# Modulation rows in column groups, input products inside the last chunks, and block 2's parameters ahead of the first rows, in an S4 block with an MLP

## The chip, the cores and the metric

The kernel runs on one core of one Trainium2 chip. The metric is the device time of one execution in microseconds (us). Engines are named as the profile names them: PE multiplies matrices, PEld loads its weights, DVE works on vectors, ACT evaluates functions and copies, POOL has little to do here, SP issues DMAs. All instructions of one engine run in their order; between engines semaphores tell when an operand is ready.

## The reference

The input `x` is 2048 × 512, `c` a vector of 512. A vector of six modulation rows is computed from `c`; the rows scale, shift and gate two halves of the block.

```python
mod = (silu(c) @ w_mod).reshape(1, 6, 1, 512)          # six rows of 512
sa, ca, ga, sb, cb, gb = rows of mod
h = layernorm(x) * (1 + ca) + sa
x = x + ga * S4(h)                                     # A part
h = layernorm(x) * (1 + cb) + sb
x = x + gb * (mish(h @ w1 + b1) @ w2)                  # B part

def S4(u):                      # L = 2048, D = 512 channels, N = 128 states
    dt = exp(log_dt); A = A_re + 1j*A_im
    K[d, l] = Re sum_n C[d, n] * exp(dt[d]*A[d, n]*l) * dt[d]*B[d, n]
    y = irfft(rfft(pad(u)) * rfft(pad(K)))[:L]         # causal convolution by FFT of length 2L
    return y + u * Dskip
```

## The kernel before

The 512 channels are four **blocks** of 128. For each block the function `params(b, stage)` (lines 233 to 298), in stages 0 to 5, turns the six parameter planes `raw[b]` (B, C, A, real and imaginary) into four planes of logarithms and angles; stages 0, 2, 3 and 5 are chains of small DVE operations, stage 1 is a logarithm and an exponential on ACT, stage 4 an arctangent on ACT. The result is split into three parts and packed in a tile `pk` (one buffer), stored to DRAM by `store_pk(b)` and read back transposed by `load_s(b)` as `S3` and `S12`. `load_params(b)` loads `raw[b]`.

The convolution kernels are then made in 32 **chunks** of 16 channels, eight per block. One chunk is, in order: `s_ang` (PE, eight matmuls into `pang`), `s_sin` (ACT, three operations into `ec`), `s_mag` and `comb` (DVE, `m` and the four products in `ec`), `s_kgen` (PE, 32 matmuls into `pkg`), `s_ks` (ACT copy `ks`), `s_skip` (DVE), `s_ka` (PE, eight matmuls into `pka`), `s_tm` (ACT copy into `gk`). The steps of one chunk lie in several rounds of the loop at lines 604 to 623: round k holds `s_kgen(k-1)`, `s_ang(k+3)`, `s_ka(k-3)` for PE and so on. Before each eight chunks a `visit(b)` changes ACT's table to exponentials, makes the coefficients `co` of eight chunks (sixteen PE matmuls `pco` and ACT operations) and changes the table back; in visit 1 ACT also does the logarithm and exponential of block 3 as its last operations.

Between these run the rest of the inputs' work: `u_load`, `u_stats`, `u_norm` (layer norm and modulation of the input, on DVE), `u_mm` (first transform, PE), `u_out` (to DRAM `ud`); `mod_mm` and `mod_out`, which make rows 0 to 2 from weights `early` loaded at the start, three rows at a time in three groups of 32 output columns of the array; `gains`, which loads these rows back from DRAM `md` on all partitions (`gs`, `ga`) for `u_norm`; and `mod_row(v)` for rows 3 to 5, one row at a time in one column group, with weights `wm` loaded inside.

**What sets the order.** Four tables, `pe`, `se`, `ve` and `vt` (lines 575 to 602), say in which round each extra step stands. Steps of `ve` are spread between the DVE operations of that round, those of `vt` follow behind. `follow` (line 103) chains everything that goes through `mm`, `act`, `V`, `A` or `load` into one written order per engine; PE's is that of the `mm` calls. DMAs issued by `nc.sync.dma_start` are placed on SP by the scheduler, by priority and by when their buffers are free. In the rows of the profile most lines are those of the helpers (L119, L141, L147, L150), so steps are told apart by tiles.

After the chunks come 16 **products** (`product(q)`, lines 654 to 672): the input's columns `ur` are loaded from `ud`, transformed (PE, `pub`; ACT copy `f`), the kernel's are transformed (PE, `pkb`), multiplied on DVE (`y`), and `inverse(q)` transforms back (PE, `pz`; ACT copy `z`; store to DRAM `zd`). The weights of the MLP are loaded and split meanwhile (`w1s`, `w1h`). The last stage reads `zd`, finishes the inverse, does the second layer norm and the MLP (`pm`, `po`).

Of the kernel before, what the change touches and what calls it, by code (L numbers as in the profile page):

```python
# [84 lines left out]
def s4_block(ctx, tc, io, out):  # L85
# [390 lines left out]
    MQ = {}  # L476

    def load_mq(w):
        for n in ("mf", "mi"):
            t = MQ[n, w] = mip.tile([P, 8, P], F32, tag=n, name=f"{n}{w}")  # L480
            nc.sync.dma_start(t.rearrange("p a b -> p (a b)"), view(io[n], w * 8 * P, [[32 * P, P], [1, 8 * P]]))

    def transform(p, q, rhs):
        for c in range(2):
            for r in range(2):
                T.matmul(p[64 * r:64 * r + 64, c, :], MQ["mf", q // 4][:, 2 * (q % 4) + r, 64 * c:64 * c + 64], rhs(r),  # L486
                         start=True, stop=True)
# [100 lines left out]
    at(se, 10, run, params(3, 4))
    at(ve, 10, params, 3, 5)
    at(se, 11, store_pk, 3)  # L590
    for n, k, d in ((0, 4, ve), (1, 7, vt), (2, 9, ve), (3, 12, ve), (4, 15, vt), (5, 17, ve), (6, 20, ve), (7, 23, vt)):
# [278 lines left out]
```

## Time and profile before

| | us |
|---|---|
| median of three runs | 761.16 (759.93 to 761.22) |
| profiled execution | 760.93 |
| its span | 759.2 |
| PE busy | 649.6 (86%) |
| DVE busy | 431.8 (57%) |
| ACT busy | 318.7 (42%) |
| chunks, first angle matmul to first product | 26.3 to 298.4 |
| products, first `pub` to the end of the stretch shown | 298.4 to 389.7 |
| MLP, last stage | 419.5 to 759.2 |

A row of the trace reads: start and duration, engine, line, operation, written tile <- read tiles, partitions × elements, count of instructions that the row joins; in brackets the idle time of the engine before the row, and what ended it. A chain row has start, length, and what the chain followed there. SPq is the queue of SP, which issues DMAs. The mean granted clock of PE over the span was 0.911 of full speed.

### The profile page before, as it was taken

What the parts mean: (1) busy time and instruction counts of PE and PEld (TensorE: products, weight loads), DVE (VectorE), ACT (ScalarE), POOL (GpSimd) and SP (SyncE); (2) the same over time, 40 slices, a digit from 0 to 9 for tenths busy, and PEclk for the clock granted to TensorE, in tenths of its full rate; (3) what the DMA queues carried; (4) which work ended last, traced back from release to release, by engine and by line L of the source; (5) the groups of instructions that cost most, each with busy time, mean ns of one, the idle gap of its engine ahead of it and who ended that gap; (6) DMA issues with size and microseconds to landing.
All of it is one profiled execution on the core that took longest, in us unless ns stands there. A gap on an engine that the chain in (4) does not pass through costs nothing.

```text
span 759.2 us, 11837 instructions
## 1 busy us (share of the span) xinstructions
PE 649.6 (86%) x4848; PEld 440.8 (58%) x4848; DVE 431.8 (57%) x813; ACT 318.7 (42%) x468; POOL 5.0 (1%) x12
## 2 busy tenths in 40 slices
PE   0319887886988999999944999999999999999996
PEld 0205654663764665233311777888778877888884
DVE  7478786999897692877637724242244424332113
ACT  2156586667867684444321621232223222322220
POOL 2000000000000000000000000000000000000000
PEclk9857796997888699999985899999999999999998
DMA  6712121322422336999449625005220400011002
GB/s 184 258 67 79 43 85 42 116 101 78 126 86 84 140 112 183 251 311 297 166 125 229 163 40 110 1 0 111 55 57 1 92 19 1 0 28 30 0 1 55
DMA packets 34218, 74.56 MB, mean 98 GB/s; under 512 B 5322, under 2 KB 9806, under 8 KB 33652
## 3 DMA queue, kind: packets, MB, share of 16 engines
q1 hardware_dynamic: 33284, 72.17, 33.0%
q10 hardware_dynamic: 576, 1.05, 0.7%
q8 instruction: 38, 0.62, 0.4%
q0 software_dynamic: 304, 0.59, 0.3%
q14 instruction: 16, 0.13, 0.1%
HBM read 49.66 MB, written 24.13 MB: 97 GB/s over the span
## 4 chain that ended last, share of the span: by engine, by line
PE 71%; DVE 14%; DMA 6%; ACT 6%; issue 2%; SPq 1%; ACTq 0%; DVEq 0%
PE pm L759 21%; PE po L776 20%; PE pang L147 5%; DVE ec L119 4%; PE pz L679 4%; PE pub L486 4%; PE pkg L147 3%; PE pkb L486 3%; DVE raw L119 3%; PE pco L147 3%; PE pka L147 2%; PE pia L724 2%; ACT co L141 2%; PE pmod L147 2%; DVE m L119 2%
## 5 line engine op out<-in xcount | busy, mean ns | idle before, releaser
L759 PE MATMUL pm<-hh,w1h 128*128 128x512 f32 x448 | 142.6, 398 | 0.7 <-ACT hh L119 0.7
L141 ACT ACTIVATE mh<-pm,b 128x512 f32<-128x512 f32 x56 | 38.6, 689 | 228.4 <-PE pm L759 228.4
L119 DVE TENSOR_TENSOR mal<-mh,mah 128x512 fp32r<-128x512 f32 x56 | 38.7, 691 | 155.7 <-ACT mah L119 155.3
L759 PEld LDWEIGHTS pm<-hh,w1h 128*128 128x128 f32 x448 | 84.8, 189 | 21.6 <-ACT hh L119 1.5
L776 PE MATMUL po<-w2h,mah 128*128 128x512 f32 x224 | 89.4, 399 | 0.0
L759 PE MATMUL pm<-hh,w1l 128*128 128x512 f32 x224 | 88.8, 397 | 0.0
L776 PE MATMUL po<-w2l,mah 128*128 128x512 f32 x224 | 88.6, 395 | 0.0
L776 PE MATMUL po<-w2h,mal 128*128 128x512 f32 x224 | 88.5, 395 | 0.0
L147 PE MATMUL pang<-ac,s 96*128 96x512 f32 x128 | 55.1, 476 | 26.3 <-DMA s<-pkd 26.3
L119 DVE TENSOR_TENSOR ec<-ec,m 128x1024 f32<-128x1024 f32 x64 | 61.1, 955 | 13.4 <-ACT ec L141 12.7
L147 PE MATMUL pco<-mc,s 64*128 64x384 f32 x64 | 32.6, 604 | 35.2 <-ACT co L141 34.4
L147 PEld LDWEIGHTS pkg<-ec 128*32 128x32 f32 x2048 | 37.6, 120 | 38.4 <-issue 31.1
L147 PE MATMUL pkg<-ec 128*32 128x64 f32 x2048 | 42.5, 241 | 18.9 <-DVE ec L119 5.9
L119 DVE TENSOR_TENSOR y<-pkb,f 128x1024 f32<-128x1024 f32 x32 | 37.7, 1220 | 24.8 <-PE pkb L486 24.8
L776 PEld LDWEIGHTS po<-w2h,mah 128*128 128x128 f32 x224 | 42.1, 188 | 14.6 <-ACT mah L119 4.9
L147 PEld LDWEIGHTS pang<-ac,s 96*128 96x128 f32 x128 | 28.9, 226 | 34.1 <-issue 27.3
L759 PEld LDWEIGHTS pm<-hh,w1l 128*128 128x128 f32 x224 | 42.5, 190 | 10.1
L776 PEld LDWEIGHTS po<-w2h,mal 128*128 128x128 f32 x224 | 42.1, 188 | 10.2
L776 PEld LDWEIGHTS po<-w2l,mah 128*128 128x128 f32 x224 | 42.1, 188 | 9.8
L147 PEld LDWEIGHTS pco<-mc,s 64*128 64x128 f32 x64 | 16.9, 269 | 50.1 <-ACT co L141 47.2
L147 PE MATMUL pang<-am,s 96*128 96x512 f32 x128 | 45.4, 441 | 0.0
L119 DVE TENSOR_TENSOR m<-co 128x1024 f32<-128x1024 f32 x32 | 39.1, 1221 | 7.3 <-ACT co L141 7.3
(96 smaller groups left out, 896.8 us busy)
## 6 DMA issues: line engine op xcount, KB each, us to landing
ud<-u SPq DMA_DIRECT2D x16, 512.0 KB, 2.7
ur<-ud SPq DMA_DIRECT2D x32, 256.0 KB, 5.1
zd<-z SPq DMA_DIRECT2D x16, 512.0 KB, 2.7
zl<-zd SPq DMA_DIRECT2D x28, 256.0 KB, 4.9
x<-in_A_u SPq DMA_DIRECT2D x32, 128.0 KB, 2.9
x<-in_A_u SPq DMA_DIRECT2D x8, 512.0 KB, 6.9
out<-ot SPq DMA_DIRECT2D x32, 128.0 KB, 2.3
w1s<-in_B_w SPq DMA_DIRECT2D x8, 448.0 KB, 6.2
```

Source lines behind the costliest of these rows:

```text
L119: ins = getattr(self.engine, name)(*a, **kw)
L141: follow("act", nc.scalar.activation(out, in_, f, **kw))
L147: follow("pe", T.matmul(out, lhsT, rhs, start=start, stop=stop))
L486: T.matmul(p[64 * r:64 * r + 64, c, :], MQ["mf", q // 4][:, 2 * (q % 4) + r, 64 * c:64 * c + 64], rhs(r), start=True, stop=True)
L679: T.matmul(p[:, r, :], mi[64 * r:64 * r + 64, q % 4, c, :], Y[q][64 * r:64 * r + 64, c, :], start=(c == 0), stop=(c == 1))
L724: T.matmul(p[64 * tl:64 * tl + 64, :], di, ZL[tt, hv][:, j % 2, tl, :], start=True, stop=True)
L759: T.matmul(p, w1[wi][:, k, fs], hh[:, hi, k, :], start=(n == 0), stop=(n == 3 * KB - 1))
L776: T.matmul(PO[tt][q], a[ai][:, P * q:P * q + P], w2[wi][:, f, :], start=(f == 0 and n == 0), stop=(f == FB - 1 and n == 2))
```

## The change

It does five things. First, `load_params(2)` stands behind `load_params(1)` on SP. On SP, at the program's start (`raw2` is block 2's parameters, `pkd` the packed store and `s3`, `s12` its read-back), before:

```order
L438 DMA x0_201<-in_A_u 64x1x512 x4
L438 DMA x1_206<-in_A_u 64x1x512 x4
L438 DMA x2_211<-in_A_u 64x1x512 x3
L150 DMA pkd_75<-pk0_183 128x1536
L438 DMA x2_211<-in_A_u 64x1x512
L632 DMA b1_3014<-in_b1 128x14
L150 DMA s3_0_193<-pkd_75 64x8x128
L150 DMA s12_0_94<-pkd_75 64x4x256
L150 DMA s12_1_95<-pkd_75 64x4x256
L150 DMA raw2_197<-in_par 128x768
L150 DMA early_85<-in_w_mod 128x2x1536 x2
```

and now:

```order
L150 DMA bdk_102<-in_bdk 128x256
L150 DMA raw1_152<-in_par 128x768
L150 DMA raw2_154<-in_par 128x768
L150 DMA da_103<-in_da 128x128
L150 DMA dtap_86<-in_dtap 4x128
L150 DMA di_104<-in_di 128x64
```

The load of `raw2` moved from behind the read-back of block 0 to the sixth place of the queue; all other loads keep their order.

Second, the arctangents of blocks 1 and 2 stand behind the first chunk's sines, stage 5 and the store of block 1 behind the second chunk's, and `u_stats(0)` goes from the set-up into round 1; `mod_mm`, `mod_out` go one round ahead. On ACT, at the start of the chunks, before:

```order
L141 ACTIVATE raw1_152<-raw1_152 128x128
L141 ACTIVATE raw2_197<-raw2_197 128x128
L119 ACTIVATE ec0_337<-pang0_319 128x2x16x32
L141 ACTIVATE ec0_337<-pang0_319 128x2x16x32
L141 ACTIVATE ec0_337<-ec0_337,halfpi_100 128x2x16x32
L119 ACTIVATE ec1_341<-pang1_328 128x2x16x32
L141 ACTIVATE ec1_341<-pang1_328 128x2x16x32
L141 ACTIVATE ec1_341<-ec1_341,halfpi_100 128x2x16x32
```

and now:

```order
L119 ACTIVATE ec0_302<-pang0_284 128x2x16x32
L141 ACTIVATE ec0_302<-pang0_284 128x2x16x32
L141 ACTIVATE ec0_302<-ec0_302,halfpi_100 128x2x16x32
L141 ACTIVATE raw1_152<-raw1_152 128x128
L141 ACTIVATE raw2_154<-raw2_154 128x128
L119 ACTIVATE ec1_308<-pang1_293 128x2x16x32
L141 ACTIVATE ec1_308<-pang1_293 128x2x16x32
L141 ACTIVATE ec1_308<-ec1_308,halfpi_100 128x2x16x32
```

The three operations of `ec0` moved ahead of the two arctangents on `raw1` and `raw2`.

Third, stage 3 of block 3's parameters goes from round 8 to round 9, stages 4 and 5 from round 10 to 11, its store to 12, and `u_norm(2)` from 9 to 10. On DVE, from the last operations of round 7's end on (`m2_8` and `ec8` belong to chunk 8), before:

```order
L119 TENSOR_TENSOR m2_8_1005<-co8_946 128x1024
L119 TENSOR_TENSOR ec8_857<-ec8_857,m2_8_1005 128x32x32
L119 TENSOR_SCALAR raw3_317<-raw3_317 128x128 x2
L119 TENSOR_TENSOR raw3_317<-raw3_317 128x256
L119 TENSOR_TENSOR raw3_317<-raw3_317 128x128
L119 SCALAR_TENSOR_TENSOR raw3_317<-raw3_317 128x128
L119 TENSOR_TENSOR m2_9_1078<-co9_953 128x1024
L119 TENSOR_TENSOR raw3_317<-raw3_317 128x128
L119 TENSOR_SCALAR raw3_317<-raw3_317 128x128
L119 TENSOR_TENSOR raw3_317<-raw3_317 128x128
L119 TENSOR_SCALAR raw3_317<-raw3_317,ldt_79 128x128
L119 TENSOR_TENSOR raw3_317<-raw3_317 128x128 x2
```

and now:

```order
L119 TENSOR_TENSOR m2_8_1005<-co8_946 128x1024
L119 TENSOR_TENSOR ec8_857<-ec8_857,m2_8_1005 128x32x32
L119 BN_STATS bst_1069<-x2_211 128x6 x2
L119 BN_STATS bst_1069<-x3_926 128x6
L119 TENSOR_TENSOR m2_9_1076<-co9_953 128x1024
L119 BN_STATS bst_1069<-x3_926 128x6
L119 BN_AGGR mv_134<-bst_1069 128x2 x2
L119 TENSOR_TENSOR ec8_857<-ec8_857,m2_8_1005 128x16x32
L119 BN_AGGR mv_134<-bst_1069 128x2 x2
L119 TENSOR_SCALAR rsq_1070<-mv_134 128x4
L119 TENSOR_SCALAR rstd_135<-rsq_1070 128x4
L119 SCALAR_TENSOR_TENSOR ec8_857<-ec8_857,m2_8_1005 128x16x32
```

The block 3 operations between the two parts of chunk 8's combination gave their place to the statistics of the inputs `x2` and `x3`.

Fourth, rows 3 to 5 are made together: `mod_piece(k)`, in rounds 27 to 30, does the matmuls of a quarter of the sum for all three rows, in three column groups of one tile `pmq`; `mod_last` copies and stores them. Their weights are loaded in pieces before (`wm_load`), the first four into the buffer of `raw`, the others into that of `u_load`.

Fifth, the matrices `mf`, `mi` are loaded from round 26 on (`second_part`), the first two product inputs in rounds 30 and 31; `pub(0)` stands in round 31 and `pub(1)` behind the last chunk, in the old PSUM pool, and the matmuls of all products go through `mm`, so in written order. On PE, at the end of the chunks, before:

```order
L147 MATMUL pka27_2858<-bdk_102,ks27_2731 64x32x4 x8
L147 MATMUL pmod5_2877<-wm50_2878,sc_133 32x512 x2
L147 MATMUL pmod5_2877<-wm52_2882,sc_133 32x512 x2
L147 MATMUL pkg30_2889<-ec30_2733 32x64 x32
L147 MATMUL pka28_2922<-bdk_102,ks28_2799 64x32x4 x8
L147 MATMUL pkg31_2939<-ec31_2801 32x64 x32
L147 MATMUL pka29_2972<-bdk_102,ks29_2867 64x32x4 x8
L147 MATMUL pka30_2985<-bdk_102,ks30_2931 64x32x4 x8
L147 MATMUL pka31_2996<-bdk_102,ks31_2981 64x32x4 x8
L486 MATMUL pub0_3041<-ur0_3038,mf0_3010 64x512 x4
L486 MATMUL pkb0_3048<-gk_635,mf0_3010 64x512 x4
L486 MATMUL pub1_3062<-ur1_3059,mf0_3010 64x512 x4
```

and now:

```order
L147 MATMUL pka27_2869<-bdk_102,ks27_2760 64x32x4 x8
L147 MATMUL pmq_2688<-wm8_2614,sc_133 32x512
L147 MATMUL pmq_2688<-wm10_2821,sc_133 32x512 x2
L147 MATMUL pkg30_2894<-ec30_2762 32x64 x32
L147 MATMUL pka28_2927<-bdk_102,ks28_2819 64x32x4 x8
L147 MATMUL pub0_2936<-ur0_2883,mf0_2621 64x512 x4
L147 MATMUL pkg31_2955<-ec31_2824 32x64 x32
L147 MATMUL pka29_2988<-bdk_102,ks29_2881 64x32x4 x8
L147 MATMUL pka30_3004<-bdk_102,ks30_2941 64x32x4 x8
L147 MATMUL pka31_3014<-bdk_102,ks31_2997 64x32x4 x8
L147 MATMUL pub1_3024<-ur1_2946,mf0_2621 64x512 x4
L147 MATMUL pkb0_3055<-gk_635,mf0_2621 64x512 x4
```

Whole rows of modulation left the place between `pka27` and `pkg30`, and a quarter of the sum for three rows stands there (three matmuls); `pub0` moved ahead of `pkg31`, `pub1` ahead of `pkb0`.

```diff
@@ -389,16 +389,27 @@
         A.copy(m[0:96], mod["p"][0:96])
         nc.sync.dma_start(md[0:3], m[0:96:32, :])
 
-    def mod_row(v):
-        p = bank(f"pmod{v}")
-        for k in range(KB):
-            if k % 2 == 0:
-                w = io4.tile([P, 2, D], F32, tag="i", name=f"wm{v}{k}")
-                nc.sync.dma_start(w, view(io["w_mod"], k * P * 6 * D + D * v, [[6 * D, P], [P * 6 * D, 2], [1, D]]))
-            mm(p[0:32, :], sc[:, k:k + 1].to_broadcast([P, 32]), w[:, k % 2], start=(k == 0), stop=(k == KB - 1))
-        m = io4.tile([P, D], F32, tag="o", name=f"mrow{v}", bufs=2)
-        A.copy(m[0:32], p[0:32])
-        nc.sync.dma_start(md[v:v + 1], m[0:1])
+    WM = {}
+
+    def wm_load(*pieces):
+        n = len(pieces)
+        t = gen.tile([P, n, D], F32, tag="raw", name="wm", bufs=1) if n > 2 else \
+            io4.tile([P, n, D], F32, tag="i", name=f"wm{pieces[0]}")
+        for i, p in enumerate(pieces):
+            WM[p] = t[:, i]
+            nc.sync.dma_start(WM[p], view(io["w_mod"], p // 3 * P * 6 * D + (3 + p % 3) * D, [[6 * D, P], [1, D]]))
+
+    def mod_piece(k):
+        if k == 0:
+            mod["q"] = psum.tile([P, 512], F32, tag="pu", name="pmq")
+        for v in range(3):
+            mm(mod["q"][32 * v:32 * v + 32, :], sc[:, k:k + 1].to_broadcast([P, 32]), WM[3 * k + v],
+               start=(k == 0), stop=(k == KB - 1))
+
+    def mod_last():
+        m = io4.tile([P, D], F32, tag="o", name="mrow2", bufs=2)
+        A.copy(m[0:96], mod["q"][0:96])
+        nc.sync.dma_start(md[3:6], m[0:96:32, :])
 
 
     def rsqrt(dst, var, n, pool, tag, V=V):
@@ -473,18 +484,37 @@
             A.copy(u[:, g], PU[n, s][g])
         nc.sync.dma_start(view(ud, 2 * (4 * n + s) * 2 * ROW, [[D, P], [4 * 2 * ROW, 2], [1, D]]), u)
 
-    MQ = {}
+    MQ, UR, FQ = {}, {}, {}
 
     def load_mq(w):
         for n in ("mf", "mi"):
-            t = MQ[n, w] = mip.tile([P, 8, P], F32, tag=n, name=f"{n}{w}")
+            t = MQ[n, w] = MQ["pool"].tile([P, 8, P], F32, tag=n, name=f"{n}{w}")
             nc.sync.dma_start(t.rearrange("p a b -> p (a b)"), view(io[n], w * 8 * P, [[32 * P, P], [1, 8 * P]]))
+
+    def second_part():
+        p0.close()
+        MQ["pool"] = left.enter_context(tc.tile_pool(name="mip", bufs=2))
+        load_mq(0)
 
     def transform(p, q, rhs):
         for c in range(2):
             for r in range(2):
-                T.matmul(p[64 * r:64 * r + 64, c, :], MQ["mf", q // 4][:, 2 * (q % 4) + r, 64 * c:64 * c + 64], rhs(r),
-                         start=True, stop=True)
+                mm(p[64 * r:64 * r + 64, c, :], MQ["mf", q // 4][:, 2 * (q % 4) + r, 64 * c:64 * c + 64], rhs(r))
+
+    def ur_load(q):
+        u = UR[q] = io4.tile([P, 2, D], F32, tag="i", name=f"ur{q}")
+        for c in range(2):
+            nc.sync.dma_start(u[64 * c:64 * c + 64].rearrange("p r d -> p (r d)"),
+                              view(ud, c * ROW + 2 * q * D, [[2 * ROW, 64], [1, 2 * D]]))
+
+    def pub(q, pool):
+        FQ[q] = pool.tile([P, 2, 512], F32, tag="pa", name=f"pub{q}", **({} if q < 2 else {"bufs": 1}))
+        transform(FQ[q], q, lambda r: UR[q][:, r, :])
+
+    def pub_out(q):
+        f = io4.tile([P, 2, D], F32, tag="o", name=f"f{q}", bufs=2)
+        A.copy(f, FQ[q])
+        FQ[q] = f
 
 
     def run(*lists):
@@ -502,6 +532,7 @@
     V.tensor_mul(sc, sc, cT)
     load(bdk, io["bdk"].rearrange("p (c x) -> p c x", c=2))
     load_params(1)
+    load_params(2)
     load(da, io["da"])
     load(dtap[0:P:32], io["dtap"].rearrange("t (k m) -> t k m", m=4))
     load(di, io["di"])
@@ -524,7 +555,6 @@
 
     store_pk(0)
     load_s(0)
-    load_params(2)
     for k in range(0, KB, 2):
         load(early[:, k:k + 2], view(io["w_mod"], k * P * 6 * D, [[6 * D, P], [P * 6 * D, 2], [1, 3 * D]]))
     for n in range(3):
@@ -534,13 +564,8 @@
     tables("natural_log_exp_and_others")
     run(params(1, 1), params(2, 1))
     tables("trig_and_small")
-    run(u_stats(0), params(1, 2), params(2, 2))
+    run(params(1, 2), params(2, 2))
     run(params(1, 3), params(2, 3))
-    run(params(1, 4), params(2, 4))
-    run(params(1, 5))
-    store_pk(1)
-    load_params(3)
-
     NG = 8 * NB
     done = set()
 
@@ -565,7 +590,11 @@
     s_ang(0)
     s_ang(1)
     s_sin(0)
+    run(params(1, 4), params(2, 4))
     s_sin(1)
+    run(params(1, 5))
+    store_pk(1)
+    load_params(3)
     run(params(2, 5))
     visit(0, {2: [lambda: step(s_mag, 0), lambda: run(comb(0))], 4: [lambda: step(s_mag, 1)]})
     store_pk(2)
@@ -577,20 +606,21 @@
     def at(d, k, f, *a):
         d.setdefault(k, []).append((f, *a))
 
-    at(pe, 1, mod_mm)
-    at(se, 2, mod_out)
+    at(pe, 0, mod_mm)
...
     at(ve, 3, gains)
     for b in range(NB - 1):
         at(se, 8 * b + 1, load_s, b + 1)
     at(ve, 2, params, 3, 0)
     at(ve, 5, params, 3, 2)
-    at(ve, 8, params, 3, 3)
...
+    at(ve, 9, params, 3, 3)
...
         at(d, k, u_norm, n)
         for s in range(2):
             t = k + 1 + s
@@ -598,10 +628,18 @@
             at(se, t + 1, u_out, n, s)
         if n + 3 < 8:
             at(se, t + 1, u_load, n + 3)
-    for v in range(3):
-        at(vt, NG - 4 + v, mod_row, 3 + v)
-
-    for k in range(NG + 3):
+    for k, pieces in (20, range(4)), (22, (4, 5)), (23, (6, 7)), (26, (8, 9)), (29, (10, 11)):
+        at(se, k, wm_load, *pieces)
+    for k in range(KB):
+        at(pe, NG - 5 + k, mod_piece, k)
+    at(se, NG - 1, mod_last)
+    at(se, NG - 6, second_part)
+    at(se, NG - 2, ur_load, 0)
+    at(se, NG - 1, ur_load, 1)
+    at(pe, NG - 1, pub, 0, psum)
+    at(se, NG, pub_out, 0)
+
+    for k in range(NG + 1):
         tc.cur_priority = 100000 + 10000 * k
         for s in [(s_kgen, k - 1), (s_ang, k + 3), (s_ka, k - 3)] + pe.get(k, []):
             step(*s)
@@ -621,13 +659,17 @@
         if k % 8 == 7 and k + 1 < NG:
             visit(k // 8 + 1)
             step(s_mag, k + 1)
+    s_skip(NG - 1)
+    for f in s_ka, s_tm:
+        f(NG - 2)
+    for f in s_ka, s_tm:
+        f(NG - 1)
+    pub(1, psum)
+    pub_out(1)
     V.on = A.on = False
 
 
     tc.cur_priority = 100000 + 10000 * (NG + 3)
-    p0.close()
-    mip = left.enter_context(tc.tile_pool(name="mip", bufs=2))
-    load_mq(0)
     b1 = keep.tile([P, FB], F32, name="b1")
     nc.sync.dma_start(b1, io["b1"])
     right.close()
@@ -654,14 +696,11 @@
     def product(q):
         if q % 4 == 0 and q < 12:
             load_mq(q // 4 + 1)
-        u = io4.tile([P, 2, D], F32, tag="i", name=f"ur{q}")
-        for c in range(2):
-            nc.sync.dma_start(u[64 * c:64 * c + 64].rearrange("p r d -> p (r d)"),
-                              view(ud, c * ROW + 2 * q * D, [[2 * ROW, 64], [1, 2 * D]]))
-        p = pair("pu", f"pub{q}", 1)
-        transform(p, q, lambda r: u[:, r, :])
-        f = io4.tile([P, 2, D], F32, tag="o", name=f"f{q}", bufs=2)
-        A.copy(f, p)
+        if q > 1:
+            ur_load(q)
+            pub(q, psum)
+            pub_out(q)
+        f = FQ[q]
         p = pair("pk", f"pkb{q}")
         transform(p, q, lambda r: gk[0][:, 2 * q + r, :])
         y = Y[q] = yp.tile([P, 2, D], F32, tag="y1", name=f"y1_{q}")
@@ -676,7 +715,7 @@
         mi = MQ["mi", q // 4].rearrange("p (q c) x -> p q c x", c=2)
         for c in range(2):
             for r in range(2):
-                T.matmul(p[:, r, :], mi[64 * r:64 * r + 64, q % 4, c, :], Y[q][64 * r:64 * r + 64, c, :],
+                mm(p[:, r, :], mi[64 * r:64 * r + 64, q % 4, c, :], Y[q][64 * r:64 * r + 64, c, :],
                          start=(c == 0), stop=(c == 1))
         z = yp.tile([P, 2, D], F32, tag="z", name=f"z{q}")
         A.copy(z, p)
```

More of the change, by code (lines that the diff above doesn't have):

```diff
@@ L578, in at @@
         d.setdefault(k, []).append((f, *a))
-    at(pe, 1, mod_mm)
-    at(se, 2, mod_out)
+    at(pe, 0, mod_mm)
+    at(se, 1, mod_out)
+    at(ve, 1, u_stats, 0)
     at(ve, 3, gains)
@@ L586, in s4_block @@
     at(ve, 5, params, 3, 2)
-    at(ve, 8, params, 3, 3)
[L588 to L591, printed above, removed]
+    at(ve, 9, params, 3, 3)
+    at(se, 11, run, params(3, 4))
+    at(ve, 11, params, 3, 5)
+    at(se, 12, store_pk, 3)
+    for n, k, d in ((0, 4, ve), (1, 7, vt), (2, 10, ve), (3, 12, ve), (4, 15, vt), (5, 17, ve), (6, 20, ve), (7, 23, vt)):
         if n % 2 == 0 and n:
-            at(ve, k - 1, u_stats, n)
+            at(ve, 8 if n == 2 else k - 1, u_stats, n)
         at(d, k, u_norm, n)
```

## The prediction

> **What bounds the kernel now.** I read the chain of waits first, then the busy times stage by stage, then the wait rows at the three places that the change touches.
>
> ```profile
> PE 71%; DVE 14%; DMA 6%; ACT 6%; issue 2%; SPq 1%; ACTq 0%; DVEq 0%
> ```
> ```profile
> 124.20:180.50 56.30, 42.89 (x666) 30.50 (x664) 55.41 (x112) 36.10 (x54) 0.00 (x0) 0.92 0.33 111
> 307.30:389.70 82.40, 80.97 (x351) 25.92 (x350) 60.90 (x68) 34.66 (x35) 0.00 (x0) 1.00 0.77 239
> 419.50:759.20 339.70, 332.69 (x1440) 261.02 (x1440) 114.07 (x211) 87.71 (x133) 0.00 (x0) 0.99 0.18 40
> ```
> (Stretch, length, then busy time of PE, PEld, DVE, ACT, POOL, PE clock, DMA share, GB/s.) In the products (307.3 to 389.7) and in the MLP after them PE is busy nearly throughout, and in the last chunks the chain goes from one PE piece to the next (rows in part 3): there only PE work taken out, or PE started earlier, counts. From 124.2 to 180.5 DVE is busy 55.41 of 56.30: what starts earlier on DVE there carries through. Before 124 waits set the time (rows in parts 1 and 2). The change takes nothing out after 307 and so can only shift that part.
>
> **Part 1, the start.** Block 2's parameters load right behind block 1's; `u_stats(0)` goes into chunk 1, the arctangents and stage 5 of block 1 behind `s_sin`; the first three modulation rows come a chunk earlier.
>
> ```profile
> 3.09 0.43 SPq L150 DMA_DIRECT2D da<-in_da  x1
> 17.38 0.34 SPq L150 DMA_DIRECT2D pkd<-pk  x1
> 22.98 0.60 SPq L150 DMA_DIRECT2D raw<-in_par  x1
> 28.46 2.98 DVE L119 TENSOR_TENSOR raw<-raw 128x256 f32<-128x256 f32 x11 [11.11 <-DMA raw<-in_par]
> 26.28 0.77 PE L147 MATMUL pang<-ac,s 96*128 96x512 f32 x1 [26.28 <-DMA s<-pkd]
> 29.39 1.06 PE L147 MATMUL pang<-ac,s 96*128 96x512 f32 x2
> 46.37 0.51 ACT L141 ACTIVATE raw<-raw 128x128 f32<-128x128 f32 x2 [12.27 <-DVE raw L119]
> 46.78 1.00 ACT L119 ACTIVATE ec<-pang 128x1024 f32<-128x1024 f32 x1
> 48.59 1.15 ACT L141 ACTIVATE ec<-ec,halfpi 128x1024 f32<-128x1024 f32 x1
> 46.71 0.62 DVE L119 SCALAR_TENSOR_TENSOR raw<-raw 128x128 f32<-128x128 f32 x2 [0.30 <-ACT raw L141]
> 55.84 1.22 DVE L119 TENSOR_TENSOR m<-co 128x1024 f32<-128x1024 f32 x1
> 69.87 1.23 DVE L119 TENSOR_TENSOR ec<-ec,m 128x1024 f32<-128x1024 f32 x1 [3.22 <-ACT ec L141]
> ```
> SP issues block 2's load at 22.98, behind the store of block 0's packed parameters and its read-back. It lands 5.5 us later (22.98 to 28.46), and DVE stands idle 11.11 for it. In the new order it takes the place of the `da` load, 3.09, and by the same latency lands near 9, before DVE reaches its first use at about 15. The new wait is the read-back: the angle matmuls of chunk 0 start when it lands, at 26.28. Six stage-0 operations of blocks 1 and 2 now stand between those of block 0's packing. By the row at 28.46 (2.98 for eleven) six are 1.6, by the short gaps between dependent operations that they can fill nothing; I charge 0.9, so the angles start at 27.2. Chunk 0's eight matmuls lie between 26.28 and about 29.9, in the middle of the row at 29.39, so 3.6: 30.8. The new ACT order puts the three sine operations of chunk 0 (2.96: from 46.78 to 48.59 + 1.15) ahead of the two arctangents: 33.8, then 0.4 (46.37 to 46.78), so 34.2. DVE's own set-up, 28.46 to 46.71 before, loses `u_stats(0)` (4.7, below) and the six operations (1.6); begun behind the packing at 18.3 (17.38 + 0.9) it is done at 18.3 + 18.25 − 6.3 = 30.2. So the sines, not DVE, decide. From the arctangent (46.71) to m(0) (55.84) there are 9.13; kept whole, this gives m(0) at 43.4, 12.4 earlier. Chunk 1's combination ends where DVE begins to wait for chunk 2's sines, 69.87 − 3.22 = 66.65, so 54.2. `u_stats(0)` is added there:
>
> ```profile
> 166.20 1.23 DVE L119 TENSOR_TENSOR ec<-ec,m 128x1024 f32<-128x1024 f32 x1
> 175.62 1.95 DVE L119 TENSOR_TENSOR ec<-ec,m 128x1024 f32<-128x1024 f32 x2
> 77.91 0.77 SPq L390 DMA_DIRECT2D md<-mrow  x1
> 83.97 0.69 DVE L119 SCALAR_TENSOR_TENSOR gs<-gs,ga 128x512 f32<-128x512 f32 x1 [4.28 <-DMA ga<-md]
> ```
> A chunk with a `u_stats` among its operations lasts 9.42 there, one without 4.69, so 4.7: chunk 2's combination starts at 58.9 instead of 69.87 and finds its sines done (its 3.22 wait goes), 11.0 earlier. Then DVE waits 4.28 at 83.97 for the gains, which come by way of DRAM 6.1 after the row's store is issued (77.91 to 83.97). DVE asks for them at 83.97 − 4.28 − 11.0 = 68.7 now. One chunk (4.69 at least) earlier, the store is issued at 77.91 − 11.0 − 4.7 = 62.2 at the latest, and the gains are there at 68.3; earlier still, since in chunk 0 only angle matmuls stand ahead of the rows on PE. **Start: 11.0 + 4.3 = 15.3.** Bounds: if the gains wait returns whole, 11.0; if the operations in front of the packing cost nothing, 16.2; if they cost 1.6 whole, 14.6.
>
> **Part 2, the first visit.** `params(3,3)` moves from chunk 8 to chunk 9, and the steps after it and `u_norm(2)` move one or two chunks.
>
> ```profile
> 122.28 0.65 ACT L141 ACTIVATE raw<-raw 128x128 f32<-128x128 f32 x2
> 122.96 0.29 DVE L119 TENSOR_TENSOR raw<-raw 128x128 f32<-128x128 f32 x1 [5.99 <-ACT raw L141]
> 132.94 1.91 PE L147 MATMUL pkg<-ec 128*32 128x64 f32 x64 [3.92 <-DVE rsq L119]
> ```
> In chunk 8 DVE waits 5.99 for the logarithm and exponential of block 3, which ACT does as the last two operations of the visit, and chunk 8's combination is queued behind. PE waits 3.92 for that later. In the new order chunk 8 carries only `u_stats(2)`, whose inputs are in place, and block 3's chain starts a chunk, 4.7 or more, later, behind the 122.28 operations. Since DVE is full from there to 180, the hole is pure gain while it can pull that whole stretch forward: **6.0**. Lower bound 0: DVE then meets something else late (PE's angles or the visit's coefficients) and the hole only moves. I take the upper end, for PE has 13.4 idle in the 56.30 and can follow.
>
> **Part 3, the last chunks.** Rows 3 to 5 in three column groups, in four pieces; `pub(0)` ahead of the last kernel-generation step.
>
> ```profile
> 72.38 3.63 PE L147 MATMUL pmod<-early,sc 128*32 128x512 f32 x24
> ```
> ```profile
> 273.01 1.10 PE pkg L147 x60
> 274.11 2.00 PE pang L147 x8
> 276.11 1.02 PE pka L147 x16
> 277.13 3.55 PE pmod L147 x8
> 288.25 3.55 PE pmod L147 x8
> 293.81 1.10 PE pkg L147 x61
> 314.80 1.87 PE pub L486 x8
> 316.67 1.72 PE pkb L486 x8
> ```
> Three rows in column groups, 24 matmul records, take 3.63 at 72.38; one row alone, 8 records, takes 3.55 (277.13 is the first, 288.25 the last of three). So the three rows fall from 3 × 3.55 = 10.65 to 3.56, 0.89 a piece. `pub(0)` adds 1.87 ahead of the last generation step. From 273.0 PE then has 4 × 0.89 + 4 × 1.10 + 2.00 + 4 × 1.02 + 1.87 = 15.9, so the last generation step starts at 288.9, not 293.8, and the three last `ka` end 1.10 + 3 × 1.02 later, at 293.0; the copy f0 stands in front of the last three gk copies on ACT, and `ka(31)` waits for a bank they free. `pub(1)` runs to 294.9.
>
> ```profile
> 300.43 1.01 ACT L119 COPY f<-pub 128x1024 f32<-128x1024 f32 x1 [0.78 <-issue]
> 302.26 2.36 DVE L119 TENSOR_TENSOR y<-pkb,f 128x1024 f32<-128x1024 f32 x2 [6.72 <-PE pkb L486]
> 305.53 1.29 DVE L119 TENSOR_TENSOR y<-y,y 128x512 f32<-128x512 f32 x2
> 307.32 1.99 PE L679 MATMUL pz<-y,mi 64*128 64x512 f32 x8
> ```
> `pub(1)`'s copy takes 1.0, to 295.95; only then is a pair of banks free for `pkb(0)`, 1.72 to 297.7; the four y operations take 3.65 (2.36 + 1.29), with 0.3 of hand-overs 301.7, and `pz(0)` starts there instead of 307.32. PE then holds `pub(2)` and `pkb(2)`, and `pz(1)` follows 5.5 (1.87 + 1.72 and its own 1.9) later at 307.2, where before it was 312.88: **5.6**. Bounds: 7.1 if the whole of the rows' saving comes through (10.65 − 3.56), 3.7 if one more 1.87 of product work has to wait for a copy. The last products of this stage are as before; PE is busy 80.97 of 82.40.
>
> **The sum.** 15.3 + 6.0 + 5.6 = 26.9. The profiled execution took 760.93 (span 759.2 and 1.7 around it), 0.23 under the median: 760.93 − 26.9 = **734.0**.
>
> **The rivals.**
>
> *R1, the hole at the first visit only moves* (740). For it: the wait names ACT, which is what the visit keeps busy, and chunk 8's coefficients and sines come from ACT too. Against it: 5.99 of DVE is idle for one named operation, and that belongs to block 3. 734 + 6.0 = 740.
>
> *R2, the start gives less* (738 to 741). The gains wait returns (+4.3, 738.3), or the read-back is delayed by block 2's load sharing the transfers, and the sines are late by some 3 more (741 with both). Against it: the load would have ended 8 us before the store at 17.38.
>
> *R3, a late load at the end* (737 to 738). Matmuls stand in order on PE, so a piece whose weights have not landed holds everything behind.
> ```profile
> DMA to landing us min/median/max: 3.7/3.9/5.2
> DMA to landing us min/median/max: 3.4/5.1/6.6
> ```
> (The modulation weights, then the product inputs.) The last weights are issued after the second piece, 278.9, and needed at 284.0, 5.1 later; the first product input after the third piece, 281.9, needed at 287.0. Median landings fit; the longest (5.2 and 6.6) miss by 0.1 and 1.5. The weights at twice their median (7.8) would miss by 2.7, which with the 1.5 behind it makes some 4: 738.
>
> *R4, the other side: slower than before.* PE falls to half clock at the new hand-over and stays there. One kind of work at two clocks:
> ```profile
> 160.36 1.96 PE L147 MATMUL pkg<-ec 128*32 128x64 f32 x64 [1.85 <-ACT gk L119]
> 174.59 1.15 PE L147 MATMUL pkg<-ec 128*32 128x64 f32 x64 [2.28 <-DVE rstd L119]
> ```
> The new order has two gaps there, about 1.1 (before `pkb(0)`) and 2.3 (before `pz(0)`, less what `pkb(1)` fills). A product at half clock costs 5.5 more; from five products on (27 of 5.5) the whole gain is gone, from six the kernel is slower, 767. Against it: the granted clock is 1.00 from 307 to 390, right behind the old hand-over, in which `pz(0)` waited for the same copy and the same y operations.
>
> [...]
>
> *R5, it does not do what it says*: the start's gain is taken back whole by the DVE-bound chunks, because PE or the read-back of block 1 is late there (734 + 15.3 = 749), or every part is (761). For it: block 1's packing now comes behind `s_sin(1)`. Against it: it starts 12 earlier all the same, and PE has 13.4 idle in that stretch.
>
> **How the numbers follow.** Forecast 734, with its own range 729 to 737 from the bounds of parts 1 and 3: 0.63. R1 0.14, R2 0.10, R3 0.06, R4 0.03, R5 0.04. The range goes down to 729 (0.9 and 1.5 from the better bounds of start and end, the rest for waits in the shifted chunks that no row prices) and up to 746, for R1 and R2 together or R1 and the lower bounds of start and end; what is left out is R4, R5 and some 0.1 that no case names. A measurement here tells 0.2%, 1.5 us, from no change. R4 gives the 0.03 for slower, half of R5 (every part lost) the 0.02 for the same; faster 0.95.
>
> **What would show it.** Right: block 2's load issued near 3 and no DVE wait of 11 for it; m(0) near 43.4; no wait for ga; no 6 us hole on DVE behind the first visit; four `pmod` pieces of 0.9 each in place of three of 3.55, and the last generation step near 293.8 − 15.3 − 6.0 − 4.9 = 267.6; `pz(0)` near 307.3 − 26.9 = 280.4. Wrong: m(0) later than 46, a wait for ga, a DVE hole in chunk 8 or 9 from ACT, PE idle for wm or ur, or product rows with a clock below 1.00.

## The result, and the profile after

The changed kernel takes 737.86 us (median of four runs, 736.62 to 739.76) against 761.19 for the kernel before beside it (759.93 to 761.60): a ratio of 0.9698, with a 95% interval of 0.967 to 0.9726. That is 23.3 us; 26.9 were forecast. The profiled execution took 739.76 and is the slowest of the four. The same kernel was profiled once more later, at 738.0 (called the control below), and the table has both.

| row (start in us) | before | changed | control | gain so far | forecast so far |
|---|---|---|---|---|---|
| gains on DVE (`gs`) | 83.97 | 68.16 | 68.09 | 15.8 / 15.9 | 15.3 |
| second coefficients of visit 2 (`pco`) | 182.35 | 162.28 | 161.03 | 20.1 / 21.3 | 21.3 |
| second coefficients of visit 3 | 241.69 | 221.23 | 219.85 | 20.5 / 21.8 | 21.3 |
| last generation step (`pkg`) | 293.74 | 269.04 | 267.59 | 24.7 / 26.2 | 26.2 |
| second inverse transform (`pz`) | 312.81 | 289.48 | 288.02 | 23.3 / 24.8 | 26.9 |
| last inverse transform | 387.75 | 365.20 | 362.96 | 22.6 / 24.8 | 26.9 |
| first matmul of the MLP (`pm`) | 419.54 | 397.29 | 394.53 | 22.3 / 25.0 | 26.9 |
| first matmul of its second part (`po`) | 429.85 | 408.46 | 406.66 | 21.4 / 23.2 | 26.9 |
| span | 759.2 | 738.0 | 736.2 | 21.2 / 23.0 | 26.9 |

Up to the last generation step the control follows the forecast to within 0.6 us. Behind it, two stretches give back: the hand-over to the products (1.4 in both) and the first matmuls of the MLP (1.8 in the control, 0.9 in the other, which also loses 0.8 within the products). The chain of waits has a smaller share of DMA than before, 4% in place of 6%:

```profile
PE 72%; DVE 15%; ACT 6%; DMA 4%; issue 2%; SPq 0%; DVEq 0%; ACTq 0%
```

These are timeline rows of the changed kernel's start:

```profile
2.63 0.91 SPq L150 DMA_DIRECT2D raw<-in_par  x2
18.14 0.33 SPq L150 DMA_DIRECT2D pkd<-pk  x1
26.78 0.77 PE L147 MATMUL pang<-ac,s 96*128 96x512 f32 x1 [26.78 <-DMA s<-pkd]
33.44 0.50 ACT L141 ACTIVATE raw<-raw 128x128 f32<-128x128 f32 x2
33.77 0.62 DVE L119 SCALAR_TENSOR_TENSOR raw<-raw 128x128 f32<-128x128 f32 x2 [4.11 <-ACT raw L141]
42.91 1.22 DVE L119 TENSOR_TENSOR m<-co 128x1024 f32<-128x1024 f32 x1
58.44 0.76 SPq L390 DMA_DIRECT2D md<-mrow  x1
68.16 0.68 DVE L119 SCALAR_TENSOR_TENSOR gs<-gs,ga 128x512 f32<-128x512 f32 x1
```

Block 2's parameters are issued with block 1's at 2.63, and the DVE wait of 11.11 for them is gone. The angles start at 26.78 (forecast 27.2); DVE then waits 4.11 for the arctangents, which stand behind the sines on ACT, so the sines decide, as was argued; m(0) is at 42.91 (43.4). The gains' operation at 68.16 waits for nothing.

At the visits and behind them, on DVE:

```profile
99.00 1.22 DVE L119 TENSOR_TENSOR m<-co 128x1024 f32<-128x1024 f32 x1 [3.13 <-ACT co L141]
128.07 0.29 DVE L119 SCALAR_TENSOR_TENSOR raw<-raw 128x128 f32<-128x128 f32 x1 [0.74 <-ACT raw L141]
182.73 1.23 DVE L119 TENSOR_TENSOR ec<-ec,m 128x1024 f32<-128x1024 f32 x1 [1.96 <-ACT ec L141]
186.65 0.69 DVE L119 BATCH_NORM_STATS2 bst<-x 128x6 f32<-128x512 f32 x1 [1.50 <-DMA x<-in_A_u]
```

The hole of 5.99 in chunk 8 is gone. What is left of it is a wait of 0.74 for block 3's arctangent in a later chunk. At the first visit DVE waits 3.13 for the coefficients, where it waited 1.86 before. The waits behind visit 2, for sines (1.96) and for an input (1.50), are not new. These are the rows of the kernel before there:

```profile
203.16 1.23 DVE L119 TENSOR_TENSOR ec<-ec,m 128x1024 f32<-128x1024 f32 x1 [2.12 <-ACT ec L141]
207.10 0.69 DVE L119 BATCH_NORM_STATS2 bst<-x 128x6 f32<-128x512 f32 x1 [1.52 <-DMA x<-in_A_u]
```

The hand-over to the products, on PE, then ACT and DVE:

```profile
252.48 1.06 PE L147 MATMUL pmq<-wm,sc 128*32 128x512 f32 x6
263.31 1.09 PE L147 MATMUL pka<-bdk,ks 128*64 128x128 f32 x16 [0.84 <-ACT gk L119]
267.22 1.89 PE L147 MATMUL pub<-ur,mf 128*64 128x512 f32 x8
269.04 1.17 PE L147 MATMUL pkg<-ec 128*32 128x64 f32 x64
273.01 1.89 PE L147 MATMUL pub<-ur,mf 128*64 128x512 f32 x8
276.05 3.65 PE L147 MATMUL pkb<-gk,mf 128*64 128x512 f32 x16 [1.16 <-ACT f L119]
282.33 2.83 PE L147 MATMUL pz<-y,mi 64*128 64x512 f32 x8 [2.62 <-DVE y L119]
285.09 2.74 PE L147 MATMUL pub<-ur,mf 128*64 128x512 f32 x8
289.48 1.99 PE L147 MATMUL pz<-y,mi 64*128 64x512 f32 x8
```
```profile
274.99 1.01 ACT L119 COPY f<-pub 128x1024 f32<-128x1024 f32 x1 [1.18 <-PE pub L147]
278.19 3.49 DVE L119 TENSOR_TENSOR y<-pkb,f 128x1024 f32<-128x1024 f32 x3 [7.36 <-PE pkb L147]
281.60 1.28 DVE L119 TENSOR_TENSOR y<-y,y 128x512 f32<-128x512 f32 x2
```

The pieces of the modulation rows are as short as forecast (six records in 1.06, or 0.88 to the next row of PE). No piece and no `pub` waits for a load. But PE now waits 1.16 for the second copy f and 2.62 for y, and after that it works at less than full clock (granted 0.68 from 282.33 to 287.67): `pz(0)` takes 2.83 and `pub(2)` 2.74 in place of 1.99 and 1.94. Three multiplications (`y<-pkb,f` x3) stand ahead of the subtraction and addition (`y<-y,y`) that `pz(0)` needs: the third belongs to product 1.

### The profile page after: what moved, and what is told of

It is laid out like the page before. It is cut to its first block, busy times and chain, and to the rows that moved or that the text cites. A ratio compares the mean times of both kernels' runs of the same rounds, so it can differ in the third digit from the quotient of the medians.

```text
span 738.0 us, 11828 instructions
## 1 busy us (share of the span) xinstructions
PE 644.8 (87%) x4848; PEld 438.9 (59%) x4848; DVE 430.2 (58%) x813; ACT 317.6 (43%) x466; POOL 5.0 (1%) x12
## 4 chain that ended last, share of the span: by engine, by line
PE 72%; DVE 15%; ACT 6%; DMA 4%; issue 2%; SPq 0%; DVEq 0%; ACTq 0%
PE pm L798 22%; PE po L815 21%; PE pang L147 5%; DVE ec L119 4%; PE pub L147 4%; PE pz L147 4%; PE pkb L147 3%; PE pkg L147 3%; PE pka L147 3%; PE pco L147 3%; PE pua L147 2%; PE pia L763 2%; DVE raw L119 2%; DVE m L119 2%; ACT ec L141 1%
## 5 line engine op out<-in xcount | busy, mean ns | idle before, releaser
L798 PEld LDWEIGHTS pm<-hh,w1h 128*128 128x128 f32 x448 | 85.3, 190 | 21.8 <-ACT hh L119 1.5
L119 DVE TENSOR_TENSOR ec<-ec,co 128x1024 f32<-128x1024 f32 x32 | 39.1, 1221 | 0.0
```

The lines of the kernel that those rows point to most:

```text
L119: ins = getattr(self.engine, name)(*a, **kw)
L798: T.matmul(p, w1[wi][:, k, fs], hh[:, hi, k, :], start=(n == 0), stop=(n == 3 * KB - 1))
```

## The experiments

All times are medians. The runs of one group (a, b, c) were made on one chip and share the runs of the kernel before (759.74, 760.60 and 759.20).

| kernel | us (range) | ratio to before, 95% |
|---|---|---|
| a1: early load alone | 749.18 (747.14 to 753.44) | 0.9874 (0.9831 to 0.9917) |
| a2: all of part 1 alone | 744.35 (742.88 to 745.45) | 0.9800 (0.9778 to 0.9822) |
| a3: changed, without part 2 | 743.15 (740.20 to 745.38) | 0.9783 (0.9750 to 0.9816) |
| a4: changed, rows 0 to 2 late again | 740.65 (738.92 to 741.82) | 0.9751 (0.9726 to 0.9775) |
| b1: changed, rows 3 to 5 one at a time | 745.78 (743.59 to 745.97) | 0.9802 (0.9781 to 0.9822) |
| b2: changed, no hoisted `pub` | 732.64 (729.90 to 736.76) | 0.9644 (0.9619 to 0.9669) |
| b3: changed, y in written order | 738.54 (737.39 to 739.57) | 0.9716 (0.9696 to 0.9735) |
| b4: changed, `pub(2)` before `pz(0)` | 735.97 (730.20 to 737.73) | 0.9672 (0.9642 to 0.9701) |
| c1: b2 and b4 together | 735.46 (733.46 to 740.10) | 0.9688 (0.9660 to 0.9716) |
| c2: changed, only `pub(0)` hoisted | 732.26 (729.74 to 734.89) | 0.9643 (0.9615 to 0.9670) |
| c3: changed, unaltered (control) | 737.63 (736.09 to 739.93) | 0.9710 (0.9686 to 0.9733) |

### a1 and a2: what the start is made of

a1 is the kernel before with one line moved; a2 has all edits of part 1, as in the diff of the change, and none of the others.

```diff
     load_params(1)
+    load_params(2)
     load(da, io["da"])
...
     load_s(0)
-    load_params(2)
```

> The kernel before with one line moved: block 2's parameters are loaded right behind block 1's, all else as before. Theory (the late load alone holds DVE): DVE's set-up, 28.5 to 46.7 before, starts behind the packing near 17.4 and ends near 35.6; the arctangents, the sines and m(0) follow 10.8 earlier (m(0) near 45.1), the wait for the gains of 4.3 stays; 761.2 - 10.8 = 750.4, or 751.6 if 1.2 are lost at the first visit as in the changed kernel's trace. Rival (something else, such as the read-back or the order of sines and arctangents, holds the start): m(0) later than 48 and over 754.

> The kernel before with all of part 1 (early load, arctangents and stage 5 behind the sines, input statistics in chunk 1, modulation rows 0 to 2 a chunk earlier) and nothing of parts 2 and 3. Theory (the parts add up): the gains' operation on DVE starts 15.8 earlier, as in the changed kernel, and 14.5 of it pass the first visit: 746.7. Rival (the hole behind the first visit takes more of it, since ACT sets that hole): 750 or more.

Timeline rows of a1, on DVE, and the row of the gains in a2:

```profile
34.65 0.62 DVE L119 SCALAR_TENSOR_TENSOR raw<-raw 128x128 f32<-128x128 f32 x2 [0.30 <-ACT raw L141]
43.79 1.22 DVE L119 TENSOR_TENSOR m<-co 128x1024 f32<-128x1024 f32 x1
72.45 0.69 DVE L119 SCALAR_TENSOR_TENSOR gs<-gs,ga 128x512 f32<-128x512 f32 x1 [4.81 <-DMA ga<-md]
```
```profile
68.20 0.68 DVE L119 SCALAR_TENSOR_TENSOR gs<-gs,ga 128x512 f32<-128x512 f32 x1
```

One moved load gives 10.6 of the 15.4 us that part 1 gives by the medians (759.74 - 749.18 and 759.74 - 744.35). By the interval of its ratio the 10.6 may be 6.3 to 12.8; in the trace a1 is 10.7 ahead at visit 2 (second coefficients at 171.62 against 182.35). In a1 the sines wait for the arctangents (34.65) and the input statistics are still in the set-up, and m(0) is only 0.9 later than in the changed kernel (43.79 against 42.91): which of the two comes first on ACT hardly matters. The remaining 4.8 agrees, within the spread of the runs, with the wait for the gains: 4.81 in a1, none in a2, where the same operation starts 4.3 earlier. So the late load held the start and the forecast's first two sizes stand. The rivals fall: a1's was m(0) later than 48 and over 754, a2's was 750 or more.

a2 came out 2.4 better than its theory (744.35 against 746.7). In its trace 14.7 are gained up to visit 2 (167.70 against 182.35), close to the 14.5 of the theory; the rest comes behind, where the stretch from visit 2 to visit 3 takes 56.5 in place of 59.3. That stretch varies with the granted clock (over the 56 us behind the second coefficients of visit 2 it is 0.91 in a2 and 0.83 in the kernel before; see c3), and part 1 moves no step in it.

### a3 and a4: the hole behind the first visit, and the gains

```diff
-    at(ve, 9, params, 3, 3)
-    at(se, 11, run, params(3, 4))
...
+    at(ve, 8, params, 3, 3)
+    at(se, 10, run, params(3, 4))
```

(a3, with the later steps of block 3 and the norm of input 2 also back; a4 has `mod_mm` in round 1 and `mod_out` in round 2.)

> The changed kernel with part 2 undone: block 3's stage 3 back in chunk 8, its later steps and the norm of input 2 back where they were. Theory (the wait for block 3's logarithm and exponential holds chunk 8): a hole of about 6 on DVE in chunk 8 is back and the time is 737.9 + 5.5 = 743.4. Rival R1 (the hole only moves): 738 to 739.

> The changed kernel with modulation rows 0 to 2 back in chunk 1 (one chunk later). Theory: DVE waits about 4.3 for the gains again and all of it reaches the end: 742.2. Rival (DVE has to wait for ACT at the first visit anyway, 3.13 in the changed kernel's trace against 1.86 before, so a part is absorbed there): 739 to 741.

One DVE row of a3, then one of a4:

```profile
107.11 0.29 DVE L119 TENSOR_TENSOR raw<-raw 128x128 f32<-128x128 f32 x1 [5.98 <-ACT raw L141]
```
```profile
70.59 0.69 DVE L119 SCALAR_TENSOR_TENSOR gs<-gs,ga 128x512 f32<-128x512 f32 x1 [2.43 <-DMA ga<-md]
```

In a3 the hole is back, 5.98, and the kernel takes 743.15, 5.3 more than the changed kernel by the medians and 6.5 by the ratios ((0.9783 - 0.9698) × 760): the hole did not only move (R1 falls). a4 comes out in the rival's range (740.65), but not for the rival's reason: the wait is 2.43, not 4.3, because the load of the gains is issued 3.7 earlier than in a1; and those 2.4 stand unabsorbed at the first visit, where the second coefficients start at 99.80, against 97.35 to 97.36 in a3, b3 and b4.

### b1 and b2: the two halves of the end

b1 puts `mod_row` back in rounds 27 to 29 in place of `mod_piece`; b2 leaves the input transforms in the product stage, with their loads still in rounds 26 to 31.

```diff
-    at(pe, NG - 1, pub, 0, psum)
-    at(se, NG, pub_out, 0)
...
-    pub(1, psum)
-    pub_out(1)
...
         if q > 1:
             ur_load(q)
-            pub(q, psum)
-            pub_out(q)
+        pub(q, psum)
+        pub_out(q)
```

> The changed kernel with rows 3 to 5 one at a time again (three times 8 matmul records of one column group each, in rounds 27 to 29), the input products where the change has them. Theory (PE sets the last chunks): PE has 10.65 - 3.56 = 7.1 more in front of the last generation step, and the time is 737.9 + 7.1 = 745.0, or less by what DVE or ACT still hold there, not under 741. Rival (other engines set the last chunks, and the rows were hidden): 738 to 739.

> The changed kernel with the first two input transforms back in the product stage, behind the last kernel transform (their inputs and matrices are still loaded ahead). Forecast's own claim (the hoist is part of a gain): about 1 to 2 slower than the changed kernel, 739 to 740. Theory from the two traces (from the last generation step to the first inverse transform it is 13.6 before and 13.3 now, with 1.87 of PE added ahead of it, and PE cools down in the wait): the hoist costs 1.6 of place and up to 1.6 of clock, so without it 734.7 to 736.3.

PE rows of b2's hand-over:

```profile
266.28 1.15 PE L147 MATMUL pkg<-ec 128*32 128x64 f32 x64 [0.19 <-DVE ks L119]
270.92 1.94 PE L147 MATMUL pub<-ur,mf 128*64 128x512 f32 x8 [0.69 <-ACT gk L119]
278.79 1.99 PE L147 MATMUL pz<-y,mi 64*128 64x512 f32 x8 [0.78 <-DVE y L119]
284.29 1.99 PE L147 MATMUL pz<-y,mi 64*128 64x512 f32 x8
```

b1: without the column groups the kernel takes 7.9 more (745.78 against 737.86, and as much by the ratios), where 7.1 were expected: PE does set the last chunks, and the groups are worth their whole price there. The trace agrees: from visit 3 to the last generation step b1 takes 55.4 and the changed kernel 47.8. b2: without the hoist it is 5.2 faster by the medians (732.64), 4.1 by the ratios ((0.9698 - 0.9644) × 760); 1.6 to 3.2 were expected. In the trace, the stretch from visit 3 to the last generation step falls from 47.81 to 46.37 (266.28 - 219.91), since no `pub(0)` stands in it, and that from there to `pz(1)` from 20.44 to 18.01; together 3.9, close to the 4.1 of the ratios. The forecast's own claim, that the hoist is part of a gain, falls.

### b3, b4, c1 and c2: why the hoist costs

b3 orders the DVE operations of products 0 and 1 as written; b4 issues `pub(2)` behind product 1, ahead of `pz(0)`; c1 does this in b2; c2 hoists only the first transform:

```diff
-    pub(1, psum)
-    pub_out(1)
...
         if q > 1:
             ur_load(q)
+        if q > 0:
             pub(q, psum)
             pub_out(q)
```

> The changed kernel with the DVE operations of the first two products in written order, so that product 0's subtraction and addition do not stand behind product 1's first multiplication. Theory (that multiplication delays the first inverse transform): it starts 1.1 earlier behind the last generation step (12.2 instead of 13.3), PE's wait of 2.62 falls to 1.5, and the time is 736.8, 735.2 if the clock stays up. Rival (the later products take it back): no difference, 737.9.

> The changed kernel with the third input transform ahead of the first inverse transform, in PE's wait of 2.62. Theory: PE works through the wait, so 1.87 leaves the path and the clock does not fall (1.64 in the changed kernel's trace): 734.4 to 736.0. [...] Other rival (product inputs or the copy are late): 737.9.

> The changed kernel without the hoisted input transforms (inputs and matrices still loaded ahead), and the third input transform ahead of the first inverse transform. Theory: the 0.78 of PE's wait in front of the first inverse transform is filled: from the last generation step to the second inverse transform 17.2 instead of 18.0, and 731.8 where the kernel without the hoist took 732.6. Rival (the copies or product inputs are late): 732.6 or more.

> The changed kernel with only the first input transform hoisted; the second one is back behind the first kernel transform. Theory (the second transform and its copy, which the first kernel transform has to wait for, cost the time, 1.87 + 1.16 + the clock): from the last generation step to the second inverse transform about 16.0 (20.4 in the changed kernel, 18.0 without any hoist), and 732.0. Rival (the first transform's place ahead of the last generation step is the costly part): 735 to 737.

DVE rows of b3, PE rows of b4, an ACT and a PE row of c1, and PE rows of c2:

```profile
279.69 2.36 DVE L119 TENSOR_TENSOR y<-pkb,f 128x1024 f32<-128x1024 f32 x2 [7.37 <-PE pkb L147]
281.96 1.08 DVE L119 TENSOR_TENSOR w1l<-w1s,w1h 128x896 fp32r<-128x896 f32 x1
282.96 1.29 DVE L119 TENSOR_TENSOR y<-y,y 128x512 f32<-128x512 f32 x2
```
```profile
270.59 1.17 PE L147 MATMUL pkg<-ec 128*32 128x64 f32 x64
283.88 1.99 PE L147 MATMUL pz<-y,mi 64*128 64x512 f32 x8 [0.91 <-DVE y L119]
287.67 1.99 PE L147 MATMUL pz<-y,mi 64*128 64x512 f32 x8
```
```profile
294.55 0.94 ACT L119 CAST w1h<-w1s 128x896 fp32r<-128x896 f32 x1 [3.08 <-DMA w1s<-in_B_w]
296.45 2.62 PE L147 MATMUL pub<-ur,mf 128*64 128x512 f32 x8 [2.15 <-ACT f L119]
```
```profile
268.08 1.17 PE L147 MATMUL pkg<-ec 128*32 128x64 f32 x64
272.91 1.94 PE L147 MATMUL pkb<-gk,mf 128*64 128x512 f32 x8 [0.69 <-ACT gk L119]
279.06 1.99 PE L147 MATMUL pz<-y,mi 64*128 64x512 f32 x8 [0.78 <-DVE y L119]
284.56 1.99 PE L147 MATMUL pz<-y,mi 64*128 64x512 f32 x8
```

b3 missed (738.54): the place that product 1's multiplication left was taken by a split of an MLP weight (`w1l`, 1.08), so `pz(0)` came just as late and PE waited 2.50 instead of 2.62. In b4 `pub(2)` fills that wait; the clock stays up, both `pz` take 1.99, and from the last generation step to `pz(1)` there are 17.1 instead of 20.4, as expected. The median (735.97) cannot tell the theory from the 1.87 alone, which would give 736.0 (737.86 - 1.87); the rows can: 3.4 are gone from the stretch, more than the 1.87 of `pub(2)`, and no transform there is slow any more. Between visits 2 and 3 this profile has the longer of two lengths (below). c1 missed (735.46, and 731.8 expected): in b2 the wait in front of `pz(0)` is only 0.78, `pub(2)` there puts `pz(0)` back by 2.0 (14.5 behind the last generation step instead of 12.5), and a few transforms later `pub` waits 2.15 for a copy that stands on ACT behind a weight that has not landed.

c2 settles it. With only the first transform hoisted the stretch is 16.5 (284.56 - 268.08; 16.0 expected), `pkb(0)` follows 0.69 after the last `ka`, no clock is lost, and the kernel takes 732.26 beside a control of 737.63 on the same chip. So it is the second transform, with its copy, that costs. Of the 3.9 by which the stretch is shorter, 2.2 lie in front of `pkb(0)` (4.8 behind the last generation step in place of 7.0) and 1.6 behind it, where `pz(0)` and `pub(2)` are no longer slow. That `pkb(0)` waits for the copy f because it needs the banks of `pub(1)` is read from the program, in which `pkb(0)` does not read that copy; no run shows it by itself. The first one, on the other hand, is worth nothing by itself, as far as two profiles tell. From visit 3 to `pz(1)` c2 takes 64.3 (284.56 - 220.25) and b2, without any, 64.4 (284.29 - 219.91): in this stretch, where PE is full (in the changed kernel busy for 45.83 of the 47.81 from visit 3 to the last generation step), work that is moved forward is paid for where it lands. c2 and b2 beat both the kernel before and the change.

### c3: the control, and the clock

> The changed kernel once more, unaltered, beside the two others on one chip: 736.6 to 739.8 as before if its spread is the clock's chance from execution to execution; at the second visit one of two lengths (58.9 or 61.6 from the second to the third visit's coefficients).

The unaltered kernel again takes 737.63, with runs from 736.09 to 739.93. A reason why its runs can differ is seen where profiles have the same work and the same wait. Here is one row of a generation step and the busy times of the stretch that follows it, first in the changed kernel, then in a3, whose program is the same up to there, and last the generation step alone in the control:

```profile
77.34 1.15 PE L147 MATMUL pkg<-ec 128*32 128x64 f32 x64 [2.45 <-DVE ec L119]
78.40:85.70 7.30, 7.30 (x34) 4.51 (x29) 7.23 (x16) 3.83 (x5) 0.00 (x0) 0.53 0.01 2
```
```profile
77.32 1.15 PE L147 MATMUL pkg<-ec 128*32 128x64 f32 x64 [2.44 <-DVE ec L119]
78.40:85.70 7.30, 5.54 (x97) 3.91 (x94) 7.23 (x16) 3.91 (x6) 0.00 (x0) 1.00 0.01 2
```
```profile
77.26 1.96 PE L147 MATMUL pkg<-ec 128*32 128x64 f32 x64 [2.44 <-DVE ec L119]
```

After the same wait, 2.45 and 2.44, the granted clock is 0.53 in one execution and 1.00 in the other; in the control even the generation step itself is slow (1.96 in place of 1.15). The changed kernel's first profile had other waits ahead of this row; the control and a3 have the same 1.83 ahead of the generation step before. The difference between the first two is worth 1.3 us here: the second coefficients of visit 1 start at 98.64 and 97.35, and DVE's wait for `co` is 3.13 and 1.87. The expected two lengths between visits 2 and 3 are there (58.8 in the control and 59.0 in the changed kernel's first profile, 61.6 in b3 and 61.7 in b4), but they are not the only ones: over all thirteen profiles the stretch takes 56.5 (a2), 58.8 to 59.6 (nine) and 61.5 to 61.7 (a4, b3 and b4). In three of them it goes with the mean granted clock. Here are the 56 us behind the second coefficients of visit 2 in a2, in the changed kernel and in b3, with clocks of 0.91, 0.85 and 0.79, where the stretch takes 56.5, 59.0 and 61.6 (stretch, length, busy times, PE clock, as in the prediction):

```profile
167.70:223.70 56.00, 48.85 (x744) 33.41 (x744) 50.29 (x80) 45.06 (x70) 0.00 (x0) 0.91 0.30 100
```
```profile
162.28:218.28 56.00, 52.44 (x744) 35.12 (x744) 50.31 (x80) 43.12 (x67) 0.00 (x0) 0.85 0.30 99
```
```profile
161.09:217.09 56.00, 52.11 (x723) 35.07 (x724) 49.12 (x79) 39.79 (x64) 0.00 (x0) 0.79 0.26 86
```

## Why the prediction was right, and where it was off

The time lies in the range, on the forecast's side, 3.9 above its point. Step by step, by the control, whose sum of differences is the same 3.9 (26.9 against 23.0 in the span):

- **The start, 15.3: measured 15.9.** The load, the read-back as the next wait, the sines as what decides and the gains all went as argued; a1 has 10.6 for the load alone, and a2 has 14.7 for the whole part up to visit 2. R2 falls.
- **The first visit, 6.0: measured 5.4**, and 0.5 more up to visit 3. The lower bound, that the hole only moves, is excluded by a3. The 0.74 wait for the arctangent of block 3 was not in the sum. That the control meets the forecast exactly at visit 2 (21.3) is luck: 0.6 too much at the start and 0.6 too little here.
- **Rows 3 to 5 and `pub(0)` up to the last generation step, 4.9: measured 4.3.** The pieces cost what was forecast; PE's new wait of 0.84 for a gk copy, which b1 with the longer rows does not have, is more than the difference. R3 falls: no piece and no input came late.
- **The hand-over, +0.7 (5.6 less 4.9): measured -1.4.** This is the step that failed. The waits were forecast as 1.1 and 2.3 and measured as 1.16 and 2.62, but the sum costs them at nothing for the clock. No run with these two waits bears that out: in the changed kernel `pz(0)` and `pub(2)` lost 1.64 to the clock, just what the rows of R4 give for two gaps (1.96 against 1.15, so 0.8 each). The other 0.5 lies ahead of `pz(0)`. The four operations of y were taken as adjacent, but a multiplication of product 1 (1.1) came ahead of product 0's subtraction; a part of it is made up, since `pz(0)` starts (282.33) before the row of y's subtraction and addition has ended (281.60 + 1.28).
- **What was not asked: whether the hoist is worth its place.** The sum took the order as it stood and priced it: with the rows' whole saving at 7.1 and the end at 5.6 it already held 1.5 against the hoist, without saying so. b2 and c2 show that it costs 4 to 5 us.
- **The MLP's first matmuls: no change forecast, 1.8 lost in the control** (12.1 from the first `pm` to the first `po`, 10.3 before). In c2 the same stretch takes 10.4, in b2 10.4, in b3 10.2. So it is no loss that goes with the change, as far as these few profiles tell; it varies with the granted clock (12.1 at 0.73 in the control, 11.2 at 0.75 in the changed kernel's first profile, 10.3 at 0.82 before).
- **R4, the half clock at the hand-over**, was right as to the place and in that the clock falls there (to 0.68 over the two transforms from 282.33 to 287.67), and wrong as to how long: it held for two transforms, not for five products or more. In the products behind it the clock was full again (1.00 from 290 to 360).
- **The chances.** Those of the six cases add up to 1.00, so there is no room among them for the 0.1 that no case names.

At the hand-over a wait of 2.50 to 2.62, with one of 1.16 that ended some 3.7 ahead of it, was followed by slow transforms: `pz(0)` took 2.83 in the changed kernel, 3.15 in the control, 2.69 in a3, 3.26 in a4 and 2.84 in b3, in place of 1.99.

## What to carry to other kernels

Moving one load forward past a store and its read-back on the same queue gave nearly half of the whole gain (10.6 of 23.3): look for loads whose place in a queue is set by program text and not by need. Here, work moved forward into a stretch where its engine is full gained nothing, and where its buffers or its copy stood in front of the chain it was meant to shorten, it cost 4 to 5 us; hoist one step, look at what it holds, and only then the next. A wait of two or three microseconds on PE should be priced with what the clock can lose behind it (here 1.64 behind 2.62), when the trace already has a row in which that happened (1.96 in place of 1.15 behind 1.85, in the kernel before).

## What was not expected of the hardware

The same work behind the same wait was granted the full clock in one execution and 0.53 in the next. Where it can be followed, this is worth 1.3 us at the first visit, and between visits 2 and 3 the profiles lie up to 5.2 us apart (56.5 to 61.7) with clocks from 0.91 to 0.79. This may be why runs of one kernel differ by 4 us here (736.1 to 739.9); it is not shown, since only two executions of the changed kernel have a profile. Differences below that have to be read from the stages. The hand-over with waits of 0.69 and 0.78 (b2, c2), or of 1.16 and 0.91 (b4), had `pz(0)` at 1.99 in the one profile taken of each; with 1.16 and then 2.50 to 2.62 it took 2.69 to 3.26 in the five profiles named above.
